# A spectral mixer and an FFN on one core: the first two token tiles normalised in transposed form, and one inverse table made by a transposing DMA

## The chip, the core and the metric

The kernel runs on one NeuronCore of one Trainium2 chip. The core has a matrix engine (TensorE, called PE in the profile, with its weight loads listed apart as PEld), a vector engine (VectorE, DVE), a scalar engine for activations and casts (ScalarE, ACT), a general engine (GpSimd, POOL) and a queue that issues DMAs (SyncE, SP). Each runs its own instructions in order and waits for the others by semaphores. SBUF is the on-chip memory, PSUM the memory that TensorE writes. The metric is the device time of one execution in microseconds (us): 160.2 us for the kernel before, the median of 3 runs (159.95 to 160.39).

## The reference

The input `x` has 2048 tokens of 512 features. Two residual blocks follow each other:

```python
h  = x + irfft2(rfft2(layernorm(x)) * (w_r + 1j * w_i))        # over tokens and features
h2 = h + (relu(layernorm(h) @ w1 + b1) ** 2) @ w2 + b2         # w1: 512 x 1792, w2: 1792 x 512
```

`layernorm` takes the mean and the variance over the 512 features of a token, with 1e-5 added to the variance and no scale or shift. Inputs, weights and the output are bf16.

## The kernel before

**Tiling.** Tokens are laid out with token p*16+g in partition p of tile g, so there are 16 tiles of 128 tokens. The 2-D transform is a chain of matrix products with tables of sines and cosines that the kernel computes itself. The tables: KF and KI along one part of the token axis, forward and inverse; EF and EI, with three slots each (sine, cosine and minus sine), along the rest of it; GF and GI along features.

**Stages.** (1) Loads, statistics of the first layernorm, tables, first product (`p1`, into `Bt`). (2) For each of eight pairs of token frequencies `pr`: the feature transform (`p2`, evicted as U), the rest of the token transform (`p3`, evicted as AB or X by ACT), then on DVE the sums X, the product m with the weights W, its complex combination Z in two halves and a fold M, then the inverse product (`p4`, with EI), evicted by ACT as T2. Pair 6 (`BY_Z`) skips the fold and multiplies Z directly. (3) For each tile the inverse feature transform. Tiles 0 and 1 take a short path, described below. The others use products into `pp` (`p5`, `p6`). (4) The FFN in five chunks of tiles: 0 to 1, 2 to 4, 5 to 8, 9 to 12, 13 to 15. For a chunk, the normalised rows are needed transposed (`UT`), with features in partitions. Each of 14 columns `f` is an up-projection (L936, PSUM tags `ph` and `sg`), a relu on ACT (`rl`, L948) and a square on DVE (`act`, L954). The down-projection (`po`, L965) follows, and DVE adds `hb`, which holds h plus the second bias (L974). Then the output is stored.

**Tiles 0 and 1 before the change.** Their inverse feature transform is in two half-size products (`d5`, L738, into `pp` and `ph`) evicted as EO. `d6` (L828 to L833) then adds x (a product of the identity with `xs`) and the products of KI with EO into one bank of tag `sg`, called `py`, with tokens in partitions. For tile 0 ACT sums the squares about the mean (L689); for tile 1 DVE uses its batch statistics (L843, L845). ACT takes the square root (L846), DVE the reciprocal and the product with minus the mean (L849, L851), and ACT (L859) or DVE (L857) writes the normalised tile `u`. Four TensorE transposes for each tile (L868) and a copy (L874) make `UT`. The mean is that of x, negated in `nm1`: the spectral branch has no constant feature column. The first two columns `f` are computed in halves, one tile each (`pf` is the first half), so that tile 0 can start before tile 1 is ready.

**The third slot of EI.** The first two slots of EI are DMA transposes of EF's, issued by SP (`tr_dma`, L453). SP's queue has, in this order: x, b1, the weights W of the spectral product with an intermediate `wx` for their reversed part, the first transpose, the two loads from `wx`, the second transpose, KI (also a transpose), and W1, W2 and b2. The third slot is the first one negated, by ACT (L482).

**What sets the order.** `Plan` is a list scheduler that runs while the program is built. Each task has an engine, a cost in us, what it reads and writes, a priority, and for buffers a tag with a number of slots. The scheduler follows its own clock and emits the instructions in the order in which they would start. For stage 2 the order is written out by hand in `MID`, one list for each of PE, ACT and DVE. Behind that the planner decides. Where its clock sees PE idle, a helper (`warm`, `bank`) puts products of a zero tile `fz` in front of the next product.

One line says how the halves of Z lie, which the change touches:

```python
ve.tensor_tensor(Z[:, :, r], T["m", pr][:, :, 0, r], T["m", pr][:, :, 1, 1 - r], (ALU.subtract, ALU.add)[r])
```

Z is `[P, u, r, 256]`: the half r has two pieces, and between them lies a piece of the other half.

Of the kernel before, what the change touches and what calls it, by code (L numbers as in the profile page):

```python
# [15 lines left out]
P = 128  # L16
# [17 lines left out]
class Plan:  # L34
# [55 lines left out]
    def run(self, line=None):  # L90
# [8 lines left out]
        while any(left.values()):  # L99
            best = None  # L100
            for e, ts in left.items():
                cand = []
                for t in ts if e not in lines else [t for t in ts if t["name"] == lines[e][0]] if lines[e] else []:
                    r = self.ready(t, e)
                    if r is None:
                        continue
                    if t["alloc"]:
                        s, _ = self.slot(t["alloc"][0])
                        if s is None:
                            continue  # L110
                        r = max(r, s)
                    r = max(r, self.free[e])
                    cand.append((r, t))
                    if r <= self.free[e] + 1e-9:
                        break
# [17 lines left out]
            if e in lines:  # L133
                lines[e].pop(0)
# [10 lines left out]
def kernel(  # L145
# [47 lines left out]
    mv2 = persist.tile([P, 2], FP32, name="mv2")  # L193
    st2 = persist.tile([P, 6], FP32, name="st2")
# [126 lines left out]
    pool(0.34, lambda: iota(idxD[:], [[1, 256]], 0, 0), 395.0, writes=["idxD"], order=[("KR", G - 1)])  # L321
# [130 lines left out]
    def tr_dma(i, dst, src, dep, prio):  # L452
        add("SP", 2.5, lambda: sy.dma_start(dst, src, transpose=True), reads=dep, writes=[("EI", i)], prio=prio, lag=(10.6, 10.4, 0, 8.0)[i])  # L453
    for i in range(2):
        tr_dma(i, EI[:, i], flat(EF[:, i]), [f"EF{i}"], 12 + i)
    tr_dma(3, KI[:], flat(KF[:]), ["KF"], 16)
    for k, (d, s) in ((0, (W1[:], B_w1.rearrange("(c p) f -> p c f", p=P))),
# [10 lines left out]
    for lt in range(4):  # L468
        pool(0.48, lambda lt=lt: gp.tensor_scalar(fiI[:, lt], idxD[:], pF[:, 5 + lt % 2:6 + lt % 2],
                                                  float((QT, HT)[lt // 2]), ALU.mult, ALU.add), 400.0,  # L470
             reads=["pF2", "idxD", ("KR", G - 1)], writes=["fiI"])
# [5 lines left out]
    def mid_tasks():  # L477
        def b1t():
            mm(sg_tile(("b1",))[:, 0:NF], lhsT=b1b[:], rhs=ident[0:NF, 0:NF], start=True, stop=True)
        add("PE", 0.07, b1t, reads=["b1b", "ident"], order=[("p3", 3)], writes=[("b1",)], prio=141.0, alloc=("sg", ("b1",)))  # L480
        act(0.19, lambda: sc.copy(b1f[:], T[("b1",)][:, 0:NF]), 142.0, reads=[("b1",)], writes=["b1f"])
        act(1.1, lambda: sc.activation(flat(EI[:, 2]), flat(EI[:, 0]), ACT.Identity, scale=-1.0), 83.0, reads=[("EI", 0)],  # L482
            order=["EF2", ("X", 0, 0)], writes=[("EI", 2)])
# [3 lines left out]
        act(1.07, lambda: sin_of(flat(GI[:]), lo(flat(fiI[:]))), 142.0, reads=["fiI"], order=[("p3", 4)], writes=["GI"])  # L487
        act(1.4, lambda: sc.activation(junk[:, 0:1], eps[:], ACT.Sqrt), 0.0, reads=["GI", "eps", ("p4", SQ)], writes=["sqrt"])

# [7 lines left out]
    for pr, first in ((0, 1), (1, 1), *((p, 0) for p in range(8))):  # L497
# [124 lines left out]
        def zz(pr=pr, r=0):  # L622
            Z = buf(fwd, ("Z", pr), "Z", [P, 2, 2, 256], BF16, 2) if r == 0 else T["Z", pr]
            ve.tensor_tensor(Z[:, :, r], T["m", pr][:, :, 0, r], T["m", pr][:, :, 1, 1 - r], (ALU.subtract, ALU.add)[r])  # L624
# [18 lines left out]
        def s4(pr, part, lts):  # L643
            key = ("p4", pr, "t", lts[0] // 2) if pr == 7 else ("p4", pr)
            pt = T[key] if part else (sg_tile if pr == 7 else mm_tile)(key)
            src = T["M" if pr and pr not in BY_Z else "Z", pr][:].rearrange("p u r (j e) -> p u r e j", e=2)
            for lt in lts:
                r, e = lt // 2, lt % 2
                k = lt - lts[0] if pr == 7 else lt
# [11 lines left out]
                else:  # L661
                    mm(o, lhsT=src[:, part, r, e, :], rhs=EI[:, 1 - part:3 - part, pr, :],
                       start=part == 0 and e == 0, stop=part == 1 and e == 1)
        for h in range(2):
            for k in range(2) if pr == 7 else (None,):
                lts = {None: range(4) if pr else (2 * h, 2 * h + 1), 0: (0, 1), 1: (2, 3)}[k]
                add("PE", 0.92 if pr in BY_Z else 0.46 if k is None else 0.23, lambda pr=pr, h=h, s4=s4, lts=lts: s4(pr, h, lts),
                    reads=[("Z", pr) if pr == 0 else ("ZM"[pr not in BY_Z] + "h" * (1 - h), pr), ("EI", 0), ("EI", 1), ("EI", 2)]
                    + [("EI", 3, pr)] * (pr in BY_Z), order=[("p4", pr, 0, k)] * h, uses=[("ZM"[pr > 0 and pr not in BY_Z], pr)],
                    writes=[("p4", pr, h, k)] + [("p4", pr)] * (k is None) + [("p4", pr, "t", k)] * (k is not None),  # L670
                    name=f"p4-{pr}-{h}" + "ab"[k] * 1 if k is not None else f"p4-{pr}-{h}", prio=z + 32 * (pr < 5),
                    alloc=(("mm", ("p4", pr)) if k is None else ("sg", ("p4", pr, "t", k))) if h == 0 else None)

        def et(eng=sc.copy, pr=pr, a=0, b=G, l0=0, l1=4):
            dst = T2[:, l0:l1, a:b, 2 * pr:2 * pr + 2, :].rearrange("p l g q s -> p l q g s")
            src = T["p4", 7, "t", l0 // 2] if pr == 7 else T["p4", pr]
            eng(dst, src[:].rearrange("p (l q g s) -> p l q g s", q=2, g=G, s=8)[:, :, :, a:b])  # L677
        if pr < 7:
            act(0.97, et, z + 3, reads=[("p4", pr)], writes=["T2", "T2a"], name=f"T2-{pr}")
        else:  # L680
            for h in range(2):
                eng = ("ACT", "DVE")[h]
                add(eng, (0.24, 0.22)[h], lambda et=et, h=h, eng=eng: et(COPY[eng], 7, 0, 2, 2 * h, 2 * h + 2), prio=z,
                    reads=[("p4", 7, "t", h)], writes=["T2a"], name=f"T2a-{h}")
                add(eng, (0.52, 0.6)[h], lambda et=et, h=h, eng=eng: et(COPY[eng], 7, 2, G, 2 * h, 2 * h + 2), prio=z + 90,
                    reads=[("p4", 7, "t", h)], order=["T2a"], writes=["T2"], name=f"T2b-{h}")

    def sq_of(src, g):
# [3 lines left out]
        "PE": "p2-2-0 p2-2-1 p3-1 p2-3-0 p2-3-1 p3-2 p2-5-0 p2-5-1 p3-3 p2-6-0 b1 p2-4-0 p2-4-1 p3-5 "  # L692
             "p2-6-1 p3-4 p4-0-0 p4-0-1 p4-1-0 p4-1-1 p2-7-0 p2-7-1 p4-2-0 p4-2-1 p3-6 p3-7 p4-3-0 "
             "p4-3-1 p4-5-0 p4-5-1 p4-4-0 p4-4-1 p4-6-0 p4-6-1 p4-7-0a p4-7-0b p4-7-1a p4-7-1b",
        "ACT": "U-2 AB-1 U-3 AB-2 U-5 AB-3 EI-2 b1f U-4 AB-5 U-6 AB-4 T2-0 T2-1 U-7 GI EI-3-6 AB-6 T2-2 "
              "AB-7 T2-3 T2-5 sqrt T2-4 T2-6 T2a-0 T2b-0",
        "DVE": "m-0-0 m-0-1 Z-0-0 Z-0-1 X-1-0 X-1-1 m-1 X-2-0 Z-1-0 Z-1-1 X-2-1 M-1-0 M-1-1 X-3-0 m-2 "
              "X-3-1 Z-2-0 Z-2-1 m-3 M-2-0 Z-3-0 Z-3-1 M-2-1 M-3-0 X-4-0 m-5 X-4-1 Z-5-0 Z-5-1 m-4 "
              "M-5-0 M-5-1 M-3-1 Z-4-0 Z-4-1 m-6 M-4-0 Z-6-0 M-4-1 m-7 Z-6-1 Z-7-0 Z-7-1 M-7-0 M-7-1 "
              "T2a-1 T2b-1",  # L700
# [6 lines left out]

    pso = ctx.enter_context(tc.tile_pool(name="pso", reuse_waits="tile", bufs=2, space=bass.MemoryType.PSUM))
    ps = ctx.enter_context(tc.tile_pool(name="ps2", reuse_waits="tile", bufs=3, space=bass.MemoryType.PSUM))
# [19 lines left out]
    z = -5000.0  # L729

    for g in range(2):
        for e in (1, 0):
            ptag = "ph" if (g, e) == (1, 0) else "pp"

            def d5(g=g, e=e, ptag=ptag):
                p = bank(("pd", g, e), ptag, 1 if ptag == "ph" else 3)
                for r in range(2):
                    mm(p[:, 0:256], lhsT=flat(T2[:, 2 * r + e, g]), rhs=GI[:, 2 * r + e, :], start=(r == 0), stop=(r == 1))  # L738
            add("PE", 0.23, d5, reads=["T2a", "GI"], order=[("pd", g, 1)] * (1 - e), writes=[("pd", g, e)],
                prio=z - 1, alloc=(ptag, ("pd", g, e)))  # L740

            def deo(eng, g=g, e=e):
                COPY[eng](EO[:, g, 1 - e], T["pd", g, e][:, 0:256])
            add(("ACT", "DVE"), (0.37, 0.36), deo, reads=[("pd", g, e)], order=[("EO", g, 1)] * (1 - e),
                writes=[("EO", g, e)], prio=z + g)

# [6 lines left out]
    UPT = ("ph", "po")  # L753

    for c, (a, b) in enumerate(CHUNKS):
# [3 lines left out]
        for g in range(a, b):  # L759
            z = late + g  # L760
            if c > 0:
# [7 lines left out]
                add("PE", 0.26, s5, reads=["T2", "GI"], order=gate(c, g - a, n), writes=[("p5", g)], prio=early + 5, alloc=("pp", ("p5", g)))  # L769
# [4 lines left out]
                act(0.37, od, z, reads=[("p5", g)], order=["una0"] * (c == 1), writes=[("od", g)], alloc=("od", ("od", g)))  # L774
# [5 lines left out]
                for i in range(2):  # L780
                    dve(0.36, lambda g=g, i=i: lv1(g, i), z, reads=[("p5", g), ("od", g)],
                        order=[("qh", g)] * i + [("un", 1)] * (c == 1),
# [40 lines left out]
        if c == 0:  # L823
            for g in range(2):
                def d6(g=g, k=0):
                    py = (bank(("py", g), "sg", 2) if k == 0 else T["py", g])[:]
# [7 lines left out]
                for k in range(3):  # L834
                    add("PE", 0.22, lambda g=g, k=k, d6=d6: d6(g, k),
                        reads=[["ident"], [("EO", g, 1), ("EI", 3)], [("EO", g, 0)]][k],
                        order=[("pd", 1, 0) if k == 0 else ("pd", g, 0)] + [("py", g, j) for j in range(k)], uses=[("py", g)],
                        writes=[("py", g, k)], name=f"py-{g}-{k}", prio=-5000.0 + g - 50 * (k == 0), alloc=("sg", ("py", g)) if k == 0 else None)
                if g == 0:
                    act(0.9, lambda: sq_of(T["py", 0][:], 0), -30.0, reads=[("py", 0, 2), "nm1", "sqrt"], writes=[("ss", 0)],  # L840
                        uses=[("py", 0)])
                else:
                    dve(0.69, lambda: ve.bn_stats(st2[:], T["py", 1][:]), -30.0, reads=[("py", 1, 2)], writes=["st2"],  # L843
                        uses=[("py", 1)])
                    dve(0.13, lambda: ve.bn_aggr(mv2[:], st2[:]), -30.0, reads=["st2"], writes=[("ss", 1)])  # L845
                act(0.3, lambda g=g: sc.activation(rs2[:, g:g + 1], mv2[:, 1:2] if g else ss2[:, 0:1], ACT.Sqrt, bias=eps[:],  # L846
# [163 lines left out]
```

## Time and profile before

| | us |
|---|---|
| median of 3 runs | 160.2 (159.95 to 160.39) |
| the profiled execution's own time | 160.21 |
| its span, from the first to the last instruction | 158.4 |
| PE busy, and its share of the span | 152.0, 96% |
| DVE busy | 119.0, 75% |
| ACT busy | 102.5, 65% |
| POOL busy | 33.1, 21% |

A busy PE is not a PE at its peak: the ends of its pipelined products are modelled, and the filler products with `fz` count as busy. The granted clock of TensorE is 1.00 throughout. The page's chain, followed back from the last instruction, gives PE 74% of the span, DVE 15%, DMA 4%. The costliest groups are the down-projection (238 products, 50.0 us), the up-projections into `sg` (37.2 us) and into `ph` (19.9 us).

By stage, from the trace: the last DMA that starts the statistics lands at about 9 us; the first products of stage 2 are at 18.6; its last inverse product starts at 45.2; the first up-projection is at 51.15; the first down-projection at about 57.5; the last one ends at about 155.4. In a timeline line the columns are start, length, engine, line, operation, what it writes and reads, partitions and columns, count, and in brackets the idle time before it with what ended it.

### The profile page before, as it was taken

The numbers are of one execution on the slowest core, as the hardware profiler recorded it, in microseconds if no ns is written. First come the engines' busy times: TensorE is split into PE (matmuls) and PEld (weight loads), VectorE is DVE, ScalarE is ACT, GpSimd is POOL, SyncE is SP. The second block draws the span as 40 slices with busy tenths as digits, with TensorE's granted clock in tenths as the row PEclk, the third lists the DMA queues.
The fourth block names the chain that finished last, engine by engine and source line by source line (L and its number), as shares of the span: only waits on it lengthen the run. The fifth ranks groups of instructions, "written<-read, shape, count | busy, mean of one in ns | idle before, by whom it ended". The sixth has DMA issues, their size and how long they took to land.

```text
span 158.4 us, 2890 instructions
## 1 busy us (share of the span) xinstructions
PE 152.0 (96%) x1027; PEld 91.9 (58%) x1027; DVE 119.0 (75%) x322; ACT 102.5 (65%) x189; POOL 33.1 (21%) x83
## 2 busy tenths in 40 slices
PE   6998999999798999999999999999999999999992
PEld 4587876787477886565544544444544444565471
DVE  5999988999867987889952989991599962285221
ACT  8989679999967887297801899530588820188000
POOL 8798700000000033022240013440002240000000
DMA  4957999994000001104132000314000312010011
GB/s 128 320 187 219 242 226 218 387 363 140 0 4 0 0 4 35 35 33 35 35 66 67 33 0 4 66 35 132 33 0 0 69 36 66 33 35 4 0 66 33
DMA packets 21017, 13.43 MB, mean 85 GB/s; under 512 B 9738, under 2 KB 19722, under 8 KB 21002
## 3 DMA queue, kind: packets, MB, share of 16 engines
q1 hardware_dynamic: 21002, 13.25, 31.3%
q8 instruction: 8, 0.13, 0.3%
q14 instruction: 7, 0.06, 0.1%
HBM read 8.92 MB, written 3.01 MB: 75 GB/s over the span
## 4 chain that ended last, share of the span: by engine, by line
PE 74%; DVE 15%; DMA 4%; issue 3%; SPq 1%; ACT 1%; POOL 0%; ACTq 0%
PE po L965 31%; PE sg L936 20%; PE ph L936 10%; DMA xs<-in_A_x_dram 4%; DVE Z L624 3%; DVE m L614 3%; DVE st L393 3%; DVE X L600 2%; PE m_p L516 2%; PE pp L788 1%; DVE M L635 1%; PE pp L795 1%; SPq L272 1%; DVE M L637 1%; PE s_p L516 1%
## 5 line engine op out<-in xcount | busy, mean ns | idle before, releaser
L965 PE MATMUL po<-W,act 128*128 128x512 bf16 (+1 forms) x238 | 50.0, 366 | 0.0
L948 ACT ACTIVATE rl<-sg,b1f 128x384 bf16<-128x384 f32 (+2 forms) x46 | 27.3, 601 | 21.9 <-PE sg L936 20.6
L936 PEld LDWEIGHTS <-W 128*128 128x128 bf16 x288 | 26.8, 98 | 19.7 <-issue 0.2
L936 PE MATMUL sg<-UT,W 128*128 128x384 bf16 (+2 forms) x184 | 37.2, 337 | 0.0
L965 PEld LDWEIGHTS <-act 128*128 128x128 bf16 x238 | 23.2, 98 | 24.0
L954 DVE TENSOR_TENSOR act<-rl 128x384 bf16<-128x384 bf16 (+2 forms) x70 | 25.0, 367 | 6.5 <-ACT rl L948 6.0
L974 DVE TENSOR_TENSOR ot<-po,hb 128x512 bf16<-128x512 f32 (+1 forms) x17 | 11.2, 658 | 20.7 <-PE po L965 20.5
L880 POOL TENSOR_SCALAR rs<-ss 128x1 f32<-128x1 f32 x14 | 6.1, 435 | 90.5 <-ACT junk L689 90.5
L948 ACT ACTIVATE rl<-ph,b1f 128x512 bf16<-128x512 f32 (+2 forms) x23 | 13.8, 602 | 10.0 <-PE ph L936 9.4
L936 PE MATMUL ph<-UT,W 128*128 128x512 bf16 (+3 forms) x96 | 19.9, 330 | 0.1
L816 DVE TENSOR_TENSOR hs<-pp,xs 128x512 bf16<-128x512 f32 x14 | 9.6, 689 | 2.3 <-PE pp L788 1.3
L689 ACT ACTIVATE junk<-hs,nm 128x512 bf16<-128x512 bf16 x14 | 10.0, 714 | 0.1
L495 PE MATMUL m_p<-U,EF 128*128 128x512 bf16 (+1 forms) x46 | 9.5, 337 | 0.0
L393 DVE BATCH_NORM_STATS2 st<-xs 128x6 f32<-128x512 bf16 x14 | 9.0, 672 | 0.6 <-DMA xs<-in_A_x_dram 0.6
L811 DVE TENSOR_TENSOR R<-q 128x127 bf16<-128x127 f32 x40 | 9.4, 283 | 0.0
L820 DVE TENSOR_TENSOR hb<-hs,b2b 128x512 f32<-128x512 bf16 x14 | 9.1, 681 | 0.0
L882 POOL TENSOR_TENSOR rs<-rs,mhalf 128x1 f32<-128x1 f32 x14 | 8.0, 569 | 1.2
L778 DVE TENSOR_TENSOR q<-pp,od 128x256 f32<-128x256 f32 x20 | 7.6, 415 | 0.0
L243 PEld LDWEIGHTS <-fz 128*128 128x128 bf16 x59 | 5.0, 113 | 4.2 <-issue 2.3
L516 PE MATMUL m_p<-GF,Bt 128*128 128x256 bf16 x56 | 7.4, 273 | 0.0
L677 ACT CAST T<-m_p 128x1024 bf16<-128x1024 f32 x7 | 7.1, 1057 | 0.5 <-PE m_p L659 0.5
L593 ACT CAST AB<-m_p 128x1024 bf16<-128x1024 f32 x7 | 7.3, 1046 | 0.0
(163 smaller groups left out, 227.6 us busy)
## 6 DMA issues: line engine op xcount, KB each, us to landing
W<-in_B_w_dram SPq DMA_DIRECT2D x2, 1792.0 KB, 10.7
out_dram<-ot SPq DMA_DIRECT2D x15, 128.0 KB, 1.8
xs<-in_A_x_dram SPq DMA_DIRECT2D x4, 256.0 KB, 3.8
xs<-in_A_x_dram SPq DMA_DIRECT2D x2, 512.0 KB, 6.7
W<-wx SPq DMA_DIRECT2D x2, 448.0 KB
W<-in_A_w_r_dram SPq DMA_DIRECT2D x1, 512.0 KB, 8.0
W<-in_A_w_i_dram SPq DMA_DIRECT2D x1, 512.0 KB, 6.4
wx<-in_A_w_r_dram SPq DMA_DIRECT2D x1, 448.0 KB
```

Source lines behind the costliest of these rows:

```text
L393: ve.bn_stats(st[:], xs[:, g, :])
L495: mm(o.rearrange("p (j i e) -> p j i e", e=2, i=RUN), lhsT=w, rhs=U[:, q, s].rearrange("p (j e i) -> p j i e", e=2, i=RUN), **k)
L516: mm(puv[:, e, :], lhsT=Bt[:, 2 * t + 1 - e, 2 * pr + q, :], rhs=gfv[:, t, :, e, :], start=(t == 0), stop=(t == 1))
L689: sc.activation(junk[:], src, ACT.Square, bias=nm1[:, g:g + 1], accum_out=ss2[:, g:g + 1])
L811: ve.tensor_tensor(o, x, y, (ALU.add, ALU.subtract, ALU.subtract, ALU.add)[k])
L816: dve(0.66, lambda g=g: ve.tensor_tensor(hs[:, g, :], T["p6", g][:], xs[:, g, :], ALU.add), z, reads=[("p6", g)], writes=[("hs", g)])
L820: add(("DVE", "POOL")[HBP], (0.62, 1.3)[HBP], lambda g=g: (ve, gp)[HBP].tensor_tensor(hb[:, g, :], hs[:, g, :], b2b[:], ALU.add), prio=lat ...
L936: mm(p[:, P * i0:P * i1], lhsT=W1[:, d, bass.ts(f, P)], rhs=T["UT", c][:, i0:i1, d, :], start=(d == 0), stop=(d == ND - 1))
L948: sc.activation(r[:, 0:P * n], T["ph", c, f][:, 0:P * n], ACT.Relu, bias=b1f[:, f:f + 1], scale=1.0)
L954: ve.tensor_tensor(t[:, f, 0:P * n], r[:, 0:P * n], r[:, 0:P * n], ALU.mult)
L965: mm(p[:, cs], lhsT=T["act", c][:, f, bass.ts(i, P)], rhs=W2[:, f, cs], start=(f == 0), stop=(f == NF - 1))
L974: ve.tensor_tensor(o[:, cs], T["po", g, h][:, cs], hb[:, g, cs], ALU.add)
```

## The change

- **Chunk 0 in transposed form.** For tiles 0 and 1 the sum of x, minus the mean and the spectral branch is accumulated with features in partitions (`yt`, one bank of tag `sg` per tile). `cen` starts the bank with a product of ones and the negated mean (`nmt`, one row of high parts and one of low parts, split by POOL in `nmh` and turned by TensorE beside b1's turn). `res` adds the transposed x, `yt6` the products of EO with KI. ACT squares it (`sq0`). Four products with a matrix of ones add the squares over the features and leave the sum in every partition. ACT takes the square root for 128 columns, DVE the reciprocal for 128 columns, and one DVE product writes `UT`. Statistics by row, the normalised `u`, the transposes and their copies are gone for these tiles. `py` remains, for `hb` alone, now in tag `po` and behind `yt`.
- **The third slot of EI** is a DMA transpose of EF's third slot, behind the second one and ahead of KI.
- **Z of pair 6** is laid out with its halves contiguous.
- **Pair 7's inverse product** goes to one two-bank `mm` tile with its outputs in another order, and its late part is evicted by DVE for both halves. `d5`, EO, `cen` and `res` move into the hand-written order of stage 2, which is new for all three engines.
- **GI** is made in two halves, the first ahead of the first U. The `idxD` iota goes to the front of POOL's queue.
- **A second hand-written order**, `DRAIN`, sets what follows stage 2 on PE, ACT and DVE. `Plan.run` leaves an engine to the planner when its list has been used up.

```diff
-    pool(0.34, lambda: iota(idxD[:], [[1, 256]], 0, 0), 395.0, writes=["idxD"], order=[("KR", G - 1)])
+    pool(0.34, lambda: iota(idxD[:], [[1, 256]], 0, 0), 1.3, writes=["idxD"])
...
     tr_dma(3, KI[:], flat(KF[:]), ["KF"], 16)
+    tr_dma(2, EI[:, 2], flat(EF[:, 2]), ["EF2"], 15)
...
+    act(0.57, lambda: sin_of(flat(GI[:, 0:2]), lo(flat(fiI[:, 0:2]))), 79.0, reads=[("fiI", 0), ("fiI", 1)], order=["Bt"], writes=["GI0"])
...
         def b1t():
-            mm(sg_tile(("b1",))[:, 0:NF], lhsT=b1b[:], rhs=ident[0:NF, 0:NF], start=True, stop=True)
+            p = sg_tile(("b1",))
+            mm(p[:, 0:NF], lhsT=b1b[:], rhs=ident[0:NF, 0:NF], start=True, stop=True)
+            for g in range(2):
+                mm(p[0:2, P + P * g:2 * P + P * g], lhsT=nmh[:, g], rhs=ident[:], start=True, stop=True)
...
-        act(1.1, lambda: sc.activation(flat(EI[:, 2]), flat(EI[:, 0]), ACT.Identity, scale=-1.0), 83.0, reads=[("EI", 0)],
-            order=["EF2", ("X", 0, 0)], writes=[("EI", 2)])
...
-        act(1.07, lambda: sin_of(flat(GI[:]), lo(flat(fiI[:]))), 142.0, reads=["fiI"], order=[("p3", 4)], writes=["GI"])
+        act(0.57, lambda: sin_of(flat(GI[:, 2:4]), lo(flat(fiI[:, 2:4]))), 142.0, reads=["fiI"], order=[("p3", 4)], writes=["GI"])
...
+        pool(0.2, lambda: gp.memset(ones[:], 1.0), 400.0, writes=["ones"])
+        pool(0.15, lambda: gp.tensor_copy(nmh[:, :, 0], nm1[:, 0:2]), 401.0, reads=["nm1"], writes=["nmh0"])
...
-            ve.tensor_tensor(Z[:, :, r], T["m", pr][:, :, 0, r], T["m", pr][:, :, 1, 1 - r], (ALU.subtract, ALU.add)[r])
+            ve.tensor_tensor(Z[:, r] if pr in BY_Z else Z[:, :, r], T["m", pr][:, :, 0, r], T["m", pr][:, :, 1, 1 - r],
+                             (ALU.subtract, ALU.add)[r])
...
-                eng = ("ACT", "DVE")[h]
...
+                eng = ("DVE", "ACT")[h]
+                add(eng, (0.22, 0.24)[h], lambda h=h, eng=eng: et7(COPY[eng], h, 0, 2), prio=z,
+                    reads=[("p4", 7, "t", h)], writes=[("T2a", h)], uses=[("p4", 7)], name=f"T2a-{h}")
+                add("DVE", 0.6, lambda h=h: et7(ve.tensor_copy, h, 2, G), prio=z + 90,
+                    reads=[("p4", 7, "t", h)], order=[("T2a", h)], writes=["T2"], uses=[("p4", 7)], name=f"T2b-{h}")
...
+    def cen(g):
+        mm(sg_tile(("yt", g))[:], lhsT=ones[0:2, :], rhs=nmt[:, g].unsqueeze(1).to_broadcast([2, ND, P]), start=True, stop=False)
+
+    def res(g):
+        for d in range(ND):
+            mm(T["yt", g][:, P * d:P * d + P], lhsT=xs[:, g, P * d:P * d + P], rhs=ident[:], start=False, stop=False)
...
     MID = {
-        "PE": "p2-2-0 p2-2-1 p3-1 p2-3-0 p2-3-1 p3-2 p2-5-0 p2-5-1 p3-3 p2-6-0 b1 p2-4-0 p2-4-1 p3-5 "
+        "PE": "p3-1 p2-2-0 p2-2-1 p2-5-0 p2-4-0 p2-5-1 p3-2 p2-4-1 p3-5 p2-3-0 p2-3-1 p3-4 p2-6-0 "
...
+             "p4-5-1 p4-4-0 p4-4-1 yt-1-0 p4-6-0 p4-6-1 p4-3-0 yt-0-0 p4-3-1 yt-0-1 p4-7-0a p4-7-0b "
+             "p4-7-1a p4-7-1b yt-1-1 pd-0-1 pd-0-0 pd-1-1 pd-1-0",
-        "ACT": "U-2 AB-1 U-3 AB-2 U-5 AB-3 EI-2 b1f U-4 AB-5 U-6 AB-4 T2-0 T2-1 U-7 GI EI-3-6 AB-6 T2-2 "
+        "ACT": "AB-1 U-2 U-5 AB-2 U-4 EI-3-6 AB-5 U-3 AB-4 U-6 AB-3 b1f nmt U-7 GI T2-2 T2-0 AB-6 T2-1 "
...
+              "T2a-0 T2b-1 EO-0-1 EO-1-1 T2b-0",
...
+                    for d in range(2):
+                        mm(o[:, d], lhsT=EO[:, g, k, P * d:P * d + P],
+                           rhs=KI[:] if k else KI[:, 0].unsqueeze(1).to_broadcast([P, 2, P]), start=False, stop=k == 1 and d == 1)
...
+                act(0.6, lambda g=g: sc.activation(flat(sq0[:, g]), T["yt", g][:], ACT.Square), -30.0, reads=[("yt", g, 3)],
+                    writes=[("sq", g)], uses=[("yt", g)])
+
+                def ssm(g=g):
+                    p = bank(("ss", g), "pp" if g else "ph", 3 if g else 1)
+                    for d in range(ND):
+                        mm(p[:, 0:P], lhsT=ones[:], rhs=sq0[:, g, d], start=d == 0, stop=d == ND - 1)
...
+                act(0.3, lambda g=g: sc.activation(rsb[:, g], T["ss", g][:, 0:P], ACT.Sqrt, bias=eps[:], scale=1.0 / D), -30.0,
+                    reads=[("ss", g), "sqrt"], writes=[("sd", 0, g)])
+                dve(0.27, lambda g=g: ve.reciprocal(rsb[:, g], rsb[:, g]), -30.0, reads=[("sd", 0, g)], writes=[("r2", 0, g)])
+
+                def ut0(g=g):
+                    u = buf(ffn, ("UT", 0), "UT", [P, 4, ND, P], BF16, 2) if g == 0 else T["UT", 0]
+                    ve.tensor_tensor(u[:, g], T["yt", g][:].rearrange("p (d c) -> p d c", c=P),
+                                     rsb[:, g].unsqueeze(1).to_broadcast([P, ND, P]), ALU.mult)
...
-                    pe.transpose(p[:, P * d:P * d + P], T["u", 0][:, g, bass.ts(d, P)], ident[:])
...
-    plan.run()
+    DRAIN = {
+        "PE": "yt-0-2 yt-0-3 yt-1-2 yt-1-3 py-1-0 ss-0 py-1-1 py-0-0 ss-1 p5-3 p5-2 py-1-2 py-0-1 p5-4 "
+             "pf-1 py-0-2 pf-0 ph-0-0 ph-0-7",
+        "ACT": "sq-0 sq-1 sd-0-0 sd-0-1 od-3 od-2 rl-0-0",
+        "DVE": "r2-0-0 UT0-0 r2-0-1 UT0-1 q-3-0 q-3-1",
+    }
+    plan.run(DRAIN)
```

## The prediction

> **What bounds the kernel now.** I read the stretches first, then the chain of waits, then VectorE's (DVE's) own timeline. Busy time of each engine in three stretches (bounds in us, length, then PE, PEld, DVE, ACT and POOL busy with counts, clock, DMA share, GB/s):
>
> ```profile
> 36.00:45.30 9.30, 8.23 (x66) 5.86 (x64) 8.19 (x17) 8.82 (x12) 0.00 (x0) 1.00 0.15 47
> 45.30:51.15 5.85, 5.30 (x65) 4.22 (x63) 4.22 (x13) 4.07 (x13) 0.00 (x0) 1.00 0.01 3
> 51.15:57.40 6.25, 6.25 (x73) 5.65 (x73) 6.12 (x19) 5.60 (x14) 0.17 (x1) 1.00 0.01 3
> ```
>
> From 51.15, where the first up-projection starts, TensorE (PE) has no gap worth naming to the end: a start x earlier with the same products behind it ends the kernel x earlier. Before it PE only looks busy: 27 of its products in the middle stretch write from `fz`, fillers (10 into `pp`, 17 into `po`). So the question is when the first up-projections can start. The chain of waits there (start, length, engine, tile, line):
>
> ```profile
> 43.92 0.43 DVE M L635
> ...
> 44.40 1.05 PE s_p L662 x8
> 45.45 0.56 PE pp L716 x10
> 46.00 0.65 PE pp L738 x6
> ...
> 48.22 0.71 DVE st L843
> ...
> 49.46 0.73 ACT u L859
> 50.19 0.05 issue
> 50.24 0.41 PE po L868 x4
> 50.65 0.02 issue
> 50.67 0.43 DVE UT L874
> 51.11 0.04 issue
> 51.15 0.38 PE ph L936 x4
> ```
>
> A latency chain, engine by engine: folded spectrum, last inverse product, T2, half-size inverse (`pp`), EO, the row sum, its variance, 1/std, normalising, four transposes, copy, first up-projection; the second tile's halves start at 51.71. Ahead of it DVE is the pacer; its timeline shows two idle gaps from 24 to 44 us (bracket: idle before, and who ended it), and later the reciprocals:
>
> ```profile
> 24.46 0.76 DVE L600 TENSOR_TENSOR X<-AB 128x512 bf16<-128x512 bf16 x2 [0.61 <-ACT AB L593]
> 25.25 1.22 DVE L614 TENSOR_TENSOR m<-X,W 128x2048 bf16<-128x2048 bf16 x1
> ...
> 42.79 1.09 DVE L624 TENSOR_TENSOR Z<-m 128x512 bf16<-128x512 bf16 x3 [0.45 <-PE m_p L659]
> ...
> 49.05 0.13 DVE L849 RECIPROCAL rs<-rs 128x1 f32<-128x1 f32 x1
> ```
>
> [...]the trace has 0.68 to 0.69 (hs, hb, ot), so I price the new UT product so. [...]the trace has 0.585 for such a cast, which I take for a Square without accumulator. [...]The trace has only one-column reciprocals (0.13 and 0.16), which cannot tell.
>
> **The change, part by part.**
>
> Third inverse table. ACT loses the 1.22 us negation (L482). SP issues a third large transpose between the second and KI: about 2.6 us of its queue (the second took 2.59), so KI, W1, W2 and b2b go out 2.6 later. In the trace they landed at 26.45, 32.4, 38.96 and 39.3; 2.6 later is still ahead of their first readers (46.9, 50.8, 57.5, 51.35). The table: issue 23.5 to 26.1, plus the 2.56 between issue end and landing of the first (19.40 to 21.96): 28.7. Its first reader, p4-0-0, stands near 31.5 behind about as many PE products as now (31.18). Hidden, with 2.8 us of cover.
>
> Middle stage. DVE has the same operations. AB-1 now comes first on ACT and PE, so X-1 loses its 0.61 wait; but m-1 needs both reversed weight tables, and the trace's landing record of the second is 25.09, against m-1's start at 25.25. Gain 0.13, not 0.7. Z of spectrum 6 gets its halves contiguous, so Z-6-1 need no longer wait for the PE product that reads the other half (in the present layout the halves interleave): gain 0.45. The new order puts a consumer right after its producer twice more (Z after m-1, M after Z); by 43.89 to 43.92 [...]0.1 each where others overlap by 0.08: about 0.17 lost. Net 0.41: M-7-1 ends at 44.27, not 44.68. ACT gains 1.22 and pays 0.37 for `nmt`; half of GI (0.61) goes into its 0.87 idle before the first U. POOL: the idxD iota (0.35) moves to the front, into its 0.64 idle before `kfq`; ones and the split means come when it has nothing until 57 us.
>
> PE extra, by the spacing at which such products start in the timeline (0.055 for 128 columns, 0.108 for 256, 0.215 for 512): two mean products 0.43, eight x products 0.44, eight KI products 0.86, eight variance products 0.44, two for the means 0.11, together 2.28, less eight transposes 0.44. The fillers (27x0.055 = 1.5) go. The mean and x products, 0.87, lie in the 1.07 us that PE idles in the 9.30 of the first stretch; the others stand ahead of the first up-projection. If those gaps closed, up to 0.9 would reach the end.
>
> Drain, from M-7-1's end at 44.27 on:
> - last inverse products: start 44.48, end 45.18 (as now: four of 0.108, the last 0.27). T2a-0 on DVE 45.10, T2a-1 on ACT 45.38 to 45.60.
> - T2b-1 (0.61) waits for T2a-1: 45.63 to 46.24, then EO of tile 0 on DVE to 46.58, the other on ACT 46.63 to 47.00. The second T2b, 0.55 on ACT now, becomes 0.61 on DVE at 46.9, where DVE waits anyway.
> - KI products of tile 0: second pair 47.11, end 47.49. Square 47.54 to 48.14.
> - variance products, four at 0.055: 48.17 to 48.56. Square root of 128 columns: 0.295 for one column; a biased ACTIVATE of 256 takes 0.47 and of 384 0.60, so 0.37: to 48.98.
> - reciprocal of 128 columns [...]0.27: to 49.28. UT product 0.66: 49.31 to 49.97.
> - tile 0's half of the first up-projection at 50.14: PE is in order and has p5-4 (needing od) in front. 51.15 before: 1.01 earlier.
> - tile 1: its square root, behind Square 1 on ACT, ends before 49.7; reciprocal 49.88, UT product 50.18 to 50.84, its halves 50.87. 51.71 before: 0.84 earlier.
>
> Behind this point both kernels owe PE the same products: the eight py products and p5-2 to p5-4 are done in both. Later chunks are reordered by the planner, but the products are the same ones, and in the trace each product behind 57 us finds its operands ready: 0. The second tile decides: 0.84, less 0.04 for two short waits. On the profiled execution (160.21 around a span of 158.4, the median 160.2): 160.2 - 0.8 = 159.4.
>
> Unknown ends: reciprocal 0.27 to 1.2[...], I take 0.27, because [...]0.13 for one column is no longer than the 0.15 of a TENSOR_SCALAR; Square 0.58 to 0.70; square root 0.30 to 0.45; landing of the reversed weights 24.4 to 25.6 (it moves both kernels nearly alike); order of later chunks -0.1 to +0.25. Without the reciprocal these give 159.0 to 159.9.
>
> **Rivals.**
> - Slow reciprocal, on the other side. [...]DVE has both in series: 49.01 to 50.21, UT 50.87; second 50.85 to 52.0, UT 52.7; halves at 52.72, 1.0 later than now. 161.3. It decides from about 0.67 each, where the 0.8 is used up. For it: [...]that DVE, the middle of three engines here, has no other work to reorder. Against: the one-column rows.
> - Late table. Beyond a landing near 32 us every us is one us at p4-0-0, whose follow-ups pace ACT and DVE; at 34 it is 161.0. For it: SP's queue is one, and the first table took 5.9 from issue to landing. Against: 2.8 us of cover.
> - The gain is eaten: PE's extra 2.3 us meets gaps that have closed, or the PE order (py and p5 in front of the first halves) holds the up-projection: 160.2. For it: PE is the engine with 96%. Against: 27 fillers go.
> - The change doesn't do what it says: Z-6-1 still waits for PE. Then 0.45 is lost and it is 159.8; it lies in the first case's range.
>
> **How the numbers follow.** A difference of 0.3%, 0.48 us, is about what a measurement of this kernel can tell from none. First case 0.60 (faster 0.49, same 0.10, slower 0.01), its own range 159.0 to 159.9. Slow reciprocal 0.32, all slower. Late table 0.04, slower. Eaten 0.04: same. Sums: faster 0.49, same 0.14, slower 0.37. The range reaches over both big cases: 159.0 to 161.5.
>
> **What would show it.** Right: no wait on PE before Z-6-1; m-1 at about 25.1; M-7-1's end near 44.3; reciprocal 0.27; first halves near 50.1 and 50.9; no PE gap over 0.3 us after 51. Wrong: a RECIPROCAL row near 1.2, PE idle about 1 us before each half; p4-0-0 waiting on a DMA; PE gaps in the later chunks.

## The result, and the profile after

The changed kernel takes 160.96 us (median, 160.84 to 161.16) against 160.19 us (159.95 to 160.39): a ratio of 1.005, 95% interval 1.0032 to 1.0067. It is 0.8 us slower where 0.8 us less was predicted. A second measurement (experiment 8) gave 160.91 against 160.36, 1.0031 (1.0015 to 1.0046). The profiled execution has 161.16 us around a span of 159.4, one us more than the span before.

Busy time in the same three stretches as before (bounds, length, then PE, PEld, DVE, ACT and POOL busy with counts, clock, DMA share, GB/s):

```profile
36.00:45.30 9.30, 9.28 (x78) 7.02 (x77) 8.42 (x18) 8.58 (x10) 0.00 (x0) 1.00 0.32 102
45.30:51.15 5.85, 5.05 (x51) 3.35 (x49) 4.00 (x8) 3.29 (x9) 0.00 (x0) 1.00 0.01 3
51.15:57.40 6.25, 5.42 (x67) 4.83 (x65) 6.15 (x18) 3.86 (x10) 0.00 (x0) 1.00 0.00 0
```

PE is full in the first stretch now (9.28 of 9.30, before 8.23), and it has 0.83 us of idle time in the third, where it had none. The chain of waits says what that idle time waits for (start, length, what):

```profile
44.28 1.06 PE m_p L676 x8
...
47.71 1.08 ACT sq L861 x2
48.79 0.36 ACT rsb L869
...
49.18 0.96 DVE rsb L871
...
50.22 0.69 DVE UT L875
50.92 0.87 DVE rsb L871
...
51.88 0.70 DVE UT L875
...
52.62 0.38 PE ph L955 x4
```

Four DVE operations stand in a row from 49.18 to 52.58: reciprocal, product, reciprocal, product. They overlap only where the second reciprocal starts 0.08 before the first product's end. The timeline gives the same reciprocals with their shape, ahead of them the end of VectorE's row in stage 2 (the last M, M-7-1, ends at 44.56), and PE's two waits for the UT products:

```profile
25.22 1.23 DVE L627 TENSOR_TENSOR m<-X,W 128x2048 bf16<-128x2048 bf16 x1 [0.45 <-DMA W<-wx]
...
42.48 0.42 DVE L651 TENSOR_TENSOR M<-Z 128x512 bf16<-128x512 bf16 x1
42.93 0.76 DVE L637 TENSOR_TENSOR Z<-m 128x512 bf16<-128x512 bf16 x2
43.80 0.42 DVE L649 TENSOR_TENSOR M<-Z 128x512 bf16<-128x512 bf16 x1
44.14 0.42 DVE L651 TENSOR_TENSOR M<-Z 128x512 bf16<-128x512 bf16 x1
...
49.18 0.95 DVE L871 RECIPROCAL rsb<-rsb 128x128 f32<-128x128 f32 x1 [1.42 <-ACT rsb L869]
...
50.83 0.94 DVE L871 RECIPROCAL rsb<-rsb 128x128 f32<-128x128 f32 x1
```

```profile
50.97 0.38 PE L955 MATMUL sg<-UT,W 128*128 128x128 bf16 x4 [0.46 <-DVE UT L875]
...
52.62 0.38 PE L955 MATMUL ph<-UT,W 128*128 128x128 bf16 x4 [0.83 <-DVE UT L875]
```

The reciprocal of 128 columns takes 0.95 us, where the prediction had 0.27. And m-1 at 25.22 waits for the reversed weights, as predicted.

To compare executions, the span can be cut at four points: the start of m-1, the end of M-7-1, the start of the second tile's halves of the first up-projection, and the end. The first moves by up to 0.9 us between executions of one kernel (experiments 10 and 12: m-1 at 25.14 behind a wait of 0.85 for a DMA, and at 24.25 without one). The next two distances repeat to 0.03 us, except where a part is changed or a sentence below says more; the last is given to 0.1 us, as the spans are. All are read from the timelines of the profiled executions; where the two groups of four halves follow each other in one row, the second starts 0.22 behind the first.

| kernel (experiment) | m-1 starts | to M-7-1's end | to the second halves | to the end |
|---|---|---|---|---|
| before | 25.25 | 19.43 | 7.03 | 106.7 |
| changed | 25.22 | 19.34 | 8.06 | 106.8 |
| changed, again (8) | 25.03 | 19.34 | 8.07 | 106.8 |
| no reciprocals (1) | 24.80 | 19.34 | 6.45 | 106.8 |
| reciprocal root on ACT (2) | 25.91 | 19.34 | 6.45 | 106.8 |
| the same, again (9) | 25.69 | 19.33 | 6.46 | 106.7 |
| before, Z layout alone (3) | 25.11 | 18.96 | 7.04 | 106.7 |
| before, table by DMA alone (5) | 25.16 | 19.43 | 7.01 | 106.8 |

From before to changed: -0.03 - 0.09 + 1.03 + 0.1 = +1.0 us, the difference of the two spans. All of the loss is in the third column.

### The profile page after: what moved, and what is told of

It is laid out like the page before. It is cut to its first block, busy times and chain, and to the rows that moved or that the text cites. A ratio compares the mean times of both kernels' runs of the same rounds, so it can differ in the third digit from the quotient of the medians.

```text
span 159.4 us, 2881 instructions
## 1 busy us (share of the span) xinstructions
PE 152.4 (96%) x1020; PEld 91.5 (57%) x1020; DVE 119.0 (75%) x316; ACT 102.9 (65%) x190; POOL 33.7 (21%) x86
## 4 chain that ended last, share of the span: by engine, by line
PE 83%; DVE 6%; DMA 3%; ACT 3%; issue 1%; SPq 1%; POOL 0%; DVEq 0%; ACTq 0%
PE po L984 30%; PE sg L955 20%; PE ph L955 10%; PE m_p L508 5%; PE m_p L529 4%; PE m_p L676 3%; DMA xs<-in_A_x_dram 3%; DVE st L396 2%; PE pp L814 1%; PE m_p L673 1%; DVE rsb L871 1%; PE pp L821 1%; DVE UT L875 1%; SPq L275 1%; ACT sq L861 1%
## 5 line engine op out<-in xcount | busy, mean ns | idle before, releaser
L967 ACT ACTIVATE rl<-sg,b1f 128x512 bf16<-128x512 f32 (+2 forms) x46 | 27.4, 602 | 19.3 <-PE sg L955 17.9
L955 PE MATMUL sg<-UT,W 128*128 128x512 bf16 (+3 forms) x188 | 37.4, 334 | 0.5 <-DVE UT L875 0.5
L955 PE MATMUL ph<-UT,W 128*128 128x384 bf16 (+3 forms) x100 | 20.5, 328 | 0.8 <-DVE UT L875 0.8
L967 ACT ACTIVATE rl<-ph,b1f 128x384 bf16<-128x384 f32 (+2 forms) x24 | 14.3, 596 | 10.8 <-PE ph L955 10.2
L911 ACT ACTIVATE u<-hs,nr,rs 128x512 bf16<-128x512 bf16 x6 | 4.9, 816 | 6.7 <-POOL nr L903 6.7
L539 ACT CAST U<-m_p 128x1024 bf16<-128x1024 f32 (+1 forms) x7 | 6.8, 967 | 0.9 <-PE m_p L529 0.9
L529 PEld LDWEIGHTS <-Bt 128*128 128x128 bf16 x64 | 6.1, 98 | 1.7 <-DVE Bt L451 0.2
```

What stands on the lines that cost most here:

```text
L529: mm(puv[:, e, :], lhsT=Bt[:, 2 * t + 1 - e, 2 * pr + q, :], rhs=gfv[:, t, :, e, :], start=(t == 0), stop=(t == 1))
L955: mm(p[:, P * i0:P * i1], lhsT=W1[:, d, bass.ts(f, P)], rhs=T["UT", c][:, i0:i1, d, :], start=(d == 0), stop=(d == ND - 1))
L967: sc.activation(r[:, 0:P * n], T["ph", c, f][:, 0:P * n], ACT.Relu, bias=b1f[:, f:f + 1], scale=1.0)
```

## The experiments

**1. The reciprocals left out.** The product now multiplies by the standard deviation, so the output is not the reference's.

```diff
-                dve(0.27, lambda g=g: ve.reciprocal(rsb[:, g], rsb[:, g]), -30.0, ...
-        "DVE": "r2-0-0 UT0-0 r2-0-1 UT0-1 q-3-0 q-3-1",
+        "DVE": "UT0-0 UT0-1 q-3-0 q-3-1",
```

The edit also raises the cost that the planner assumes for the UT product from 0.66 to 1.03 us. The order of the instructions behind the second halves is that of the changed kernel on PE, ACT and DVE, here and in experiment 2.

> The changed kernel without its two wide reciprocals: the products with the row multiply by the standard deviation, so the output is not the reference's. Theory A (the two reciprocals of 0.95 us in series are the whole loss): first halves at about 50.0 us and 50.6 us instead of 50.97 and 52.62, time 158.9 to 159.3 us. Rival B (the loss is PE's 2.3 us of added products or their order, or the new order of the later chunks): the halves still come late, or PE has gaps behind 57 us, and the time stays at 160.2 us or more.

Measured: 159.07 us (158.96 to 159.58) against 160.35, 0.9931 (0.9905 to 0.9957). The halves are at 49.92 and 50.59, 1.6 us nearer to M-7-1's end than in the changed kernel (6.45 for 8.06). The profiled execution also has m-1 0.42 earlier, which the reciprocals have nothing to do with. Rival B falls: PE's added products and the later chunks are all still there. DVE's and PE's timelines:

```profile
48.76 1.35 DVE L875 TENSOR_TENSOR UT<-s_yt,rsb 128x512 bf16<-128x512 f32 x2 [1.42 <-ACT rsb L869]
```

```profile
47.94 0.38 PE L867 MATMUL ph<-sq,ones 128*128 128x128 bf16 x4 [0.25 <-ACT sq L861]
...
49.92 0.39 PE L955 MATMUL sg<-UT,W 128*128 128x128 bf16 x4
...
50.37 0.61 PE L955 MATMUL ph<-UT,W 128*128 128x128 bf16 x8
```

The two UT products now follow each other without a gap, and PE shows no wait from 47.94 to the halves: the sums, `p5`, `py` and the halves stand one behind the other. With the reciprocals gone, PE's own row is the next bound (experiment 11).

**2. Root and reciprocal in one activation.** ScalarE's absolute reciprocal square root takes the place of the square root, both here and in the early one-column activation (L496) that stands behind the load of its table.

```diff
-  act(0.3, lambda g=g: sc.activation(rsb[:, g], T["ss", g][:, 0:P], ACT.Sqrt, bias=eps[:], scale=1.0 / D), ...
-  dve(0.27, lambda g=g: ve.reciprocal(rsb[:, g], rsb[:, g]), ...
+  act(0.3, lambda g=g: sc.activation(rsb[:, g], T["ss", g][:, 0:P], ACT.Abs_reciprocal_sqrt, bias=eps[:], scale=1.0 / D), ...
```

> The changed kernel with square root and reciprocal in one ScalarE activation (absolute reciprocal square root of the 128 columns, 0.37 us as the square root takes now), no VectorE reciprocal. Theory A: the same as without the reciprocals, 158.9 to 159.3 us, so faster than the kernel before. Rival B: 160.2 us or more. If this function costs ScalarE more than the square root (say 0.7 us), some 159.7 us.

Measured: 159.17 us against 160.35, 0.9938 (0.9921 to 0.9955). The function costs ACT what the square root does (0.37 us at 48.78 in the changed kernel):

```profile
49.47 0.37 ACT L869 ACTIVATE rsb<-ph,eps 128x128 f32<-128x128 f32 x1
```

Its table load is 1.28 us at 40.18, as the square root's was (1.28 at 39.87), and the distances are those of experiment 1. So the rest of the change, with this one operation exchanged, is 0.6% faster than the kernel before. (The profiled execution was the slowest of the 15, 160.23 us, with m-1 only at 25.91.)

**3. The layout of Z alone,** on the kernel before.

```diff
-ve.tensor_tensor(Z[:, :, r], T["m", pr][:, :, 0, r], ...
+ve.tensor_tensor(Z[:, r] if pr in BY_Z else Z[:, :, r], T["m", pr][:, :, 0, r], ...
```

> The kernel before with one part of the change alone: the halves of Z of spectrum 6 lie contiguous. Theory A (the wait of 0.45 us before Z-6-1 is given back only in part by other pairs): no wait there, M-7-1 ends at about 44.25 instead of 44.68, first halves at 50.7 us, time 159.75 us. Rival: DVE then waits elsewhere (for PE or for its own results), and the time stays at 160.2.

Measured: 159.73 us against 160.35, 0.9961 (0.9948 to 0.9974). DVE's timeline, where the wait of 0.45 before Z-6-1 stood:

```profile
40.98 1.21 DVE L614 TENSOR_TENSOR m<-AB,W 128x2048 bf16<-128x2048 bf16 x1
42.12 1.09 DVE L624 TENSOR_TENSOR Z<-m 128x512 bf16<-128x512 bf16 x3
43.31 0.43 DVE L635 TENSOR_TENSOR M<-Z 128x512 bf16<-128x512 bf16 x1
```

The three halves of Z start 0.07 before m-7's end, and M-7-1 ends 18.96 behind m-1's start, 0.47 less than before. In the changed kernel the same layout comes with a new order, and there only 0.09 of it is left. Experiments 6, 7 and 10 ask why.

**4. The reciprocal by width,** on scratch at the end of the changed kernel.

```diff
+    for n in (1, 32, 64, 128, 256, 512):
+        ve.reciprocal(pb[:, 0:n], pa[:, 0:n])
```

> The changed kernel with VectorE reciprocals of 1, 32, 64, 128, 256 and 512 fp32 columns, one of 128 bf16 columns, and products of 128 and 256 fp32 columns, all on scratch at the very end (the time is longer by their sum). If the reciprocal costs a fixed number of cycles per element, about 6.4 us per 1000 columns plus 0.13 us: 0.33, 0.54, 0.95, 1.77 and 3.4 us. If 0.95 us is a fixed start cost of a wide form, all are near 0.9 us.

```profile
157.39 0.55 DVE L1012 RECIPROCAL pb<-pa 128x64 f32<-128x64 f32 x1
...
157.98 0.95 DVE L1012 RECIPROCAL pb<-pa 128x128 f32<-128x128 f32 x1
...
158.97 1.75 DVE L1012 RECIPROCAL pb<-pa 128x256 f32<-128x256 f32 x1
...
160.75 3.35 DVE L1012 RECIPROCAL pb<-pa 128x512 f32<-128x512 f32 x1
```

The time of this single execution, 168.62 us, is longer by the added operations, as expected. One column takes 0.155 us and 32 take 0.35; from 64 columns on each doubling adds 0.40, 0.80 and 1.60. That is 6.25 ns for each column on top of 0.15. A bf16 input of 128 columns also takes 0.95. A product of 128 fp32 columns takes 0.29. The cost goes by columns, and one-column rows (0.13 to 0.16) say nothing of it.

**5. The third table by DMA alone,** on the kernel before: ACT's negation out, the transpose in.

```diff
+    tr_dma(2, EI[:, 2], flat(EF[:, 2]), ["EF2"], 15)
...
-        act(1.1, lambda: sc.activation(flat(EI[:, 2]), flat(EI[:, 0]), ACT.Identity, scale=-1.0), ...
```

> The kernel before with another part of the change alone: the third inverse table is turned by DMA, and ScalarE loses its 1.22 us negation. As predicted (hidden: the table lands before its first reader at 31.2 us, and ScalarE is not what the end waits for): M-7-1's end within 0.1 us of the kernel before, counted from m-1's start (19.43 us), time 160.2 to 160.4 us. Rival (late table): the first inverse product waits for a DMA, and the time grows by that wait, to 161 us. Other rival (ScalarE was the hidden bound of the middle): 0.3 us or more faster.

Measured: 160.26 us against 160.19, 1.0004 (0.999 to 1.0017). From m-1 to M-7-1 it is 19.43 us, and PE reads the table at 31.08 straight behind its other products. Both rivals fall: neither is the table late, nor was ACT the hidden bound.

**6. The middle's old orders,** with experiment 2's activation. VectorE, ScalarE and TensorE get the lists of the kernel before, with spectrum 1's column product and cast first and the new products (`yt`, `pd`) put in.

```diff
-        "DVE": "... m-1 Z-1-0 Z-1-1 M-1-0 X-2-0 X-2-1 M-1-1 m-2 m-5 ... m-6 Z-3-1 Z-6-0 M-3-0 Z-6-1 m-7 M-3-1 Z-7-0 ...
+        "DVE": "... m-1 X-2-0 Z-1-0 Z-1-1 X-2-1 M-1-0 M-1-1 X-3-0 m-2 ... m-6 M-4-0 Z-6-0 M-4-1 m-7 Z-6-1 Z-7-0 ...
```

> The changed kernel with the reciprocal square root on ScalarE (as in the second experiment) and the middle's orders of the kernel before on VectorE, ScalarE and TensorE, except that the column product and the cast of spectrum 1 stay first. Theory (the changed order on VectorE gives back 0.38 of the 0.47 us that the layout of Z gains): from m-1's start to M-7-1's end 18.95 us instead of 19.34, time 158.8 us against 159.2 us. Rival (the 0.38 us is not the order but TensorE's added products in the middle): still 19.3 us, with waits for TensorE, and 159.2 us or more.

Measured: 160.41 us against 160.19, 1.0009 (1.0 to 1.0019). This is a miss on both sides: from m-1 to M-7-1 it takes 20.08 us. DVE's timeline shows three waits that the theory did not have:

```profile
26.74 0.43 DVE L613 TENSOR_TENSOR X<-AB 128x512 bf16<-128x512 bf16 x1 [0.63 <-ACT AB L606]
...
33.09 0.76 DVE L637 TENSOR_TENSOR Z<-m 128x512 bf16<-128x512 bf16 x2 [0.30 <-PE m_p L669]
...
46.36 0.22 DVE L693 CAST T<-m_p 128x64 bf16<-128x64 f32 x1 [1.39 <-PE m_p L676]
```

With the cast of spectrum 1 first on ACT, that of spectrum 2 comes later than the old DVE list wants it: it ends at 26.71, and X-2-0 starts at 26.74. And behind M-7-1 the last inverse product is late by another 0.6 (1.39 for 0.81), since two groups of `yt` products stood ahead of it on PE (44.73 to 45.28). The orders of the three engines belong together, and the experiment does not answer its question.

**7. Two pairs pulled apart** in the changed order, with experiment 2's activation. Spectra 3 and 6 are exchanged on PE and ACT to match. A pair here is an operation on VectorE that stands directly behind the one whose result it reads.

```diff
-        "DVE": "... Z-1-0 Z-1-1 M-1-0 X-2-0 X-2-1 M-1-1 ... M-3-0 Z-6-1 m-7 M-3-1 Z-7-0 ...
+        "DVE": "... Z-1-0 Z-1-1 X-2-0 M-1-0 X-2-1 M-1-1 ... M-3-0 M-3-1 m-7 Z-6-1 Z-7-0 ...
```

> As the sixth, from the other side: the changed kernel's own middle orders with the reciprocal square root, and on VectorE only two moves, X-2-0 between Z-1 and M-1 and M-3-1 ahead of m-7 with Z-6-1 behind it (the products of spectrum 6 and 3 exchanged on TensorE to match). Theory: each pair that is pulled apart saves 0.1 us, 19.1 us from m-1 to M-7-1, time 159.0 us. Rival: TensorE, which is busy 9.28 of 9.30 us in this stretch, now holds the last products: no gain, 159.2 us or more.

Measured: 160.06 us against 160.19, 0.9996 (0.9986 to 1.0005). Theory and rival each had one part right: M-7-1 ends 19.10 us behind m-1's start, 0.24 less, but the last inverse product comes later, and the kernel is 0.9 us slower than in experiment 2. PE's and DVE's timelines:

```profile
42.15 0.49 PE L246 MATMUL m_p<-fz 128*128 128x128 bf16 x6 [0.52 <-ACT T L690]
```

```profile
43.69 0.42 DVE L651 TENSOR_TENSOR M<-Z 128x512 bf16<-128x512 bf16 x1
45.95 0.23 DVE L693 CAST T<-m_p 128x64 bf16<-128x64 f32 x1 [1.84 <-PE m_p L676]
```

DVE waits 1.84 us for the last inverse product instead of 0.81. The products of spectrum 6, later in PE's list, stand ahead of it. The rival's reason, a full PE, is not what the trace shows: from 41.63 on PE waits 0.52 us for a T2 cast of ScalarE, and then six fillers of the planner take it to 42.48. These 0.85 us account for the delay of the last inverse products, which start 19.87 us behind m-1 for 19.06 in the changed kernel.

**8 and 9. The changed kernel and experiment 2, side by side.**

> The changed kernel itself once more, beside the next two on one chip. 160.9 to 161.1 us, a ratio of 1.003 to 1.007 to the kernel before. From m-1's start to M-7-1's end 19.34 us again, and 8.06 us from there to the second tile's halves.

> The kernel of the second experiment once more: 159.1 to 159.3 us, 1.8 us below the changed kernel, of which 1.6 are the shorter way from M-7-1's end to the second tile's halves (8.06 to 6.45 us). If the earlier difference came from the chip or from DMA arrivals of the inputs, it shrinks to 1.5 us or less here.

Measured: 160.91 us and 159.44 us, against 160.36 for the kernel before: 1.0031 (1.0015 to 1.0046) and 0.994 (0.9921 to 0.9958). The second is a little above the 159.1 to 159.3 that were expected. The distances repeat to 0.01. The medians differ by 1.5 and not 1.8, so by the expectation a part of the earlier difference came from the chip or the input's arrival. The two profiled executions differ in the arrival: m-1 starts at 25.69 in that of 9 (it waits 1.47 for the DMA) and at 25.03 in that of 8. Whether this holds for the medians is not shown.

**10 and 12. One pair pulled apart** in the kernel of experiment 2: X-2-0 between Z-1 and M-1, no other move.

> The same with one move on VectorE alone, X-2-0 between Z-1 and M-1, which pulls one dependent pair apart. If only VectorE paces the middle, 19.24 us from m-1 to M-7-1 instead of 19.34, and 0.1 us less in the time, too little for a verdict; if TensorE or the casts hold the last product, no change.

> The kernel of the tenth experiment again, beside the eleventh: 159.15 us, 6.45 us from M-7-1's end to the second tile's halves.

Measured: 159.15 us, 0.9921 (0.9893 to 0.9949), and again 159.26, 0.9933 (0.9913 to 0.9953). In the first profile m-1 to M-7-1 is 19.22 us, the 0.1 less that was expected. In the second it is 19.36, no gain: there m-1 started early, at 24.25, and X-2-0 came 0.14 later behind Z-1 than in the first. It starts just behind the end of its cast on ACT (26.30):

```profile
25.28 1.02 ACT L606 CAST AB<-m_p 128x1024 bf16<-128x1024 f32 x1
```

```profile
26.33 0.43 DVE L613 TENSOR_TENSOR X<-AB 128x512 bf16<-128x512 bf16 x1
```

All later operations keep those 0.14. Also there the last inverse product came 0.14 behind what M-7-1 alone would give (6.60 instead of 6.45). So PE and the casts are within 0.15 us of VectorE in the middle. The difference to experiments 2 and 9 is inside the intervals.

**11. Products moved forward in the drain,** on experiment 10.

```diff
-        "PE": "yt-0-2 yt-0-3 yt-1-2 yt-1-3 py-1-0 ss-0 py-1-1 py-0-0 ss-1 p5-3 p5-2 ...
+        "PE": "yt-0-2 yt-0-3 yt-1-2 yt-1-3 py-1-0 py-1-1 ss-0 py-0-0 p5-3 ss-1 p5-2 ...
```

> The kernel of the tenth experiment with two groups of products moved forward on TensorE in the drain: py-1-1 ahead of ss-0 and p5-3 ahead of ss-1. Theory (with the reciprocals gone, TensorE's own row of products from ss-0 on is what the first up-projections wait for): the products fill the 0.25 us wait for the first Square, the second tile's halves come 0.2 us earlier (6.25 us behind M-7-1's end instead of 6.45), time 0.2 us lower, 158.9 us. Rival (the latency chain of Square, sum, root and product still sets it): 6.45 us and no change.

Measured: 159.0 us (158.5 to 159.07) against 160.29, 0.9899 (0.9876 to 0.9923), the lowest median of the series. In the profile of experiment 10 PE waits for the first Square; in that of 11 it does not:

```profile
48.16 0.38 PE L867 MATMUL ph<-sq,ones 128*128 128x128 bf16 x4 [0.25 <-ACT sq L861]
```

```profile
48.10 0.39 PE L867 MATMUL ph<-sq,ones 128*128 128x128 bf16 x4
```

From the T2a cast (45.16 and 45.08) to the second halves (50.81 and 50.53) it is 5.65 and 5.45 us: the 0.2 that was expected. Experiment 12 has 5.65 too. From M-7-1's end it is 6.41 and not 6.25, since here too the last inverse product was 0.15 late; and M-7-1 ends 19.35 behind m-1's start, as in experiment 12. That TensorE's row of products is the next bound is shown by the profiles; the gain in the medians, 0.15 to 0.26, is too small for the intervals.

## Why the prediction was wrong

**The step that failed is the reciprocal in the drain:** for 128 columns the prediction had 0.27. It takes 0.95 us, 0.15 and 6.25 ns for each column (experiment 4). The two stand in series on VectorE, so 2 x 0.68 = 1.36 us was missing from the sum. The second halves started at 52.62, 1.75 us behind the predicted 50.87: 1.36 for the reciprocals, 0.29 because M-7-1 ended later (the middle stage, below), and 0.10 net for the rest of the drain, which was 0.12 shorter ahead of the first reciprocal and 0.22 longer between it and the halves. The prediction had both ends of this term, 0.27 and 1.2, and took the low one. Both were the author's estimates, which no trace showed: the kernel before has only reciprocals of one column (0.13 and 0.16). The argument from the rows of one column was empty: 0.155 for one column and 0.95 for 128 go together.

**The rival "slow reciprocal" is what happened.** The prediction gave it a chance of 0.32, and its range, 159.0 to 161.5, covers it. It decides from about 0.67 us each, and 0.95 is past that. It gave 52.72 for the second halves at 1.2 us each, and 52.62 was measured. That they are so near is partly luck: at 0.95 each the rival's own sum would give 52.22, and the 0.40 that is missing are the later M-7-1 and the rest of the drain. Experiments 1 and 2 show that the reciprocals alone turn a gain into a loss. They do not show that the forecast was right without them: 8.06 less 1.36 is 6.70, for 7.03 before, which with the 0.12 of the middle stage makes an estimate of about 0.4 us faster, not 0.8.

The other steps:

- **Third table: right.** Hidden, alone (experiment 5) and in the change. The landing records put it at 27.12, against an estimate of 28.7; its first reader, p4-0-0, starts at 31.59 behind other products. The weights W1 and W2 and b2b land 1.3 to 2.9 us later than before, unnoticed.
- **X-1 and m-1: right.** X-1's wait is gone, and m-1 waits for the second reversed weight table until 25.22 (25.12 predicted). Experiments 1 to 12 have m-1 between 24.25 and 25.91, so what this part is worth changes with the landing.
- **Z-6-1: right in place, wrong in the sum.** No wait for PE stands there, and alone it is worth 0.47 (0.45 predicted). The price of the new order was put at 0.17 for two dependent pairs; it is 0.38 (0.47 alone, 0.09 left). M-7-1 ended at 44.56, not 44.27. The timeline shows where: Z-1 starts 0.03 behind m-1's end, M-1-0 0.03 behind Z-1's, Z-7-0 0.03 behind M-3-1's, where independent operations overlap by 0.08, so 0.11 each and 0.33 together. Two of these three were in the prediction; the last 0.05 is not traced to a place. M-7-0 starts 0.11 behind Z-7's end, for 0.04 before, but this comes with the layout and not with the order: in experiment 3 it is 0.10. Pulling two pairs apart gave 0.24 (experiment 7), and one gave 0.12 in experiment 10 but nothing in 11 and 12. That Z-7-0 waits for M-3-1 because it reuses the buffer of Z-3 is argued from the order of allocation; shown is only that it no longer waits when M-3-1 comes earlier.
- **PE's added products: half right.** They went into the gaps and cost nothing in the changed kernel. But they used the gaps up (9.28 of 9.30 us): in experiments 11 and 12 the last inverse product came 0.15 us behind what M-7-1 allowed.
- **Drain up to the reciprocal: right.** Square, sum and root were at 3.15, 3.80 and 4.22 us behind M-7-1's end (3.27, 3.90 and 4.34 predicted; the root counted from its start at 48.78), with 0.37 for a root of 128 columns and 0.69 for the UT product. The Square of 512 columns, priced by the ScalarE cast of 512 columns from PSUM (0.585 before), takes 0.594, and the UT product was priced by `hs`, `hb` and `ot` (0.68 to 0.69 before).
- **Later chunks: right.** From the second halves to the end it is 106.8 us, for 106.7 before.
- **Three sums that do not come out, none of which carries the forecast.** Four products of 0.108 from 44.48 with 0.27 for the last end at 45.07, not 45.18 (T2a-0 at 45.10 fits 45.07). The late table at 34 us would give 159.4 + 2 = 161.4 by its own rule, not 161.0. In the slow rival the second reciprocal would end at 52.05, not 52.0.

## What to carry to other kernels

Price a VectorE reciprocal by its columns (6.25 ns each here, on top of 0.15 us), and not by the row of a narrow one: turning a statistic from one column into a broadcast row of 128 made two cheap operations (0.13 and 0.16 us) expensive (0.95 each). When an estimate has two ends and they lie on both sides of "faster", the whole forecast rests on that choice, and evidence that cannot tell the ends apart (here, rows of one column) must not move it. After a bound is removed, look how far the next ones are: here PE and the casts were within 0.15 us of VectorE, so moves on VectorE alone gained 0.1 us or nothing.

## What the runs showed of the hardware

- The VectorE reciprocal takes 0.155, 0.35, 0.55, 0.95, 1.75 and 3.35 us for 1, 32, 64, 128, 256 and 512 fp32 columns: 6.25 ns per column (experiment 4). With a bf16 input 128 columns take 0.95 too.
- ScalarE's absolute reciprocal square root of 128 PSUM columns takes 0.37 us, the same as its square root, and its table load the same 1.28 us (experiment 2 and the changed kernel).
- In the changed kernel five VectorE operations directly behind their producers start 0.03 to 0.11 us after the producer's end (Z-1 at 26.48 for 26.45, M-1-0 at 27.27 for 27.24, the UT products at 50.22 for 50.13 and 51.88 for 51.77, M-7-0 at 43.80 for 43.69). Two that read nothing of the operation ahead start 0.07 and 0.08 before its end (Z-6-1 at 42.12 for 42.19 in experiment 3, m-2 at 28.62 for 28.70 in the changed kernel).
